# Block-sparse attention and a SwiGLU FFN on one core: all scores on four 32-row tiles, instruction order written by hand, narrower first and last FFN chunks, rms_g applied to x

## The chip, the cores and the metric

The kernel runs on one core of a Trainium2 chip. The metric is the device time of one execution in microseconds (us). Each number below is the median of several executions, and each comparison was made on one chip, with the kernel before run beside the other kernel.

The engines are named as the profile names them. PE is TensorE (matmul), and PEld is its weight load, which overlaps PE. DVE is VectorE, ACT is ScalarE, POOL is GpSimd, and SP is SyncE. "Clock" is the share of full speed that TensorE was granted, as the profile reports it.

## The reference

It is attention over 4 batches, 8 heads, 768 positions and 64 columns. Each query may see only the 6 best blocks of 32 keys. An upper bound built from each block's minimum and maximum ranks the blocks. A gated FFN with RMS norm on 3072 tokens follows.

```python
k_min, k_max = k_chunks.min(axis=3), k_chunks.max(axis=3)           # 24 blocks of 32 keys
ub = sum_d max(q * k_min, q * k_max)                                # causal: later blocks are out
top_chunks = argsort(ub)[..., -6:]
scores = where(selected & causal, q @ k.T / sqrt(64), -1e9)
attn = softmax(scores);  x = (attn @ v) as 3072 x 512
xn = x / rms(x) * rms_g
out = (silu(xn @ w_gate) * (xn @ w_val)) @ w_out                    # 512 -> 1536 -> 512
```

## The kernel before

A *quad* is four heads of one batch (eight quads, numbered 0 to 7). A *unit* is a quad, 256 queries and 256 keys (six per quad, 48 in all). A *slice* is one piece of FFN work: either eight matmuls into `gp` and `vp` and their gating (`gated`), or twelve matmuls into one output tile (`project`). The loop over units puts two slices between the attention steps, so that TensorE has work while the softmax is under way. The parts that matter, cut:

```python
    psS = ... bufs=3 (scores)   psV = ... bufs=1 (values)   psF = ... bufs=4 (FFN and the rest)
    NTILED = NG                     # only quads 0 and 1 use row tiles

    # scores of quads 0 and 1: two heads at a time, each on 32 rows (two halves of d, then the mask)
            for t in range(3):
                for hl in range(2):
                    r = slice(32 * a, 32 * (a + 1))
                    nc.tensor.matmul(o[...], kb_[r, t, ks], qb_[r, t, qs:qs + qn], ...)
    # scores of quads 2 to 7: 88 rows a head (64 of d, 24 of the mask); moved there by DMA
                for dh in range(2):
                    for a in range(4):
                        nc.sync.dma_start(out=dst[bi][32 * dh:32 * (dh + 1), a, :],
                                          in_=hb[32 * a:32 * (a + 1), dh, :])

    # the FFN: chunks of 512 tokens; w_gate and w_val are scaled by rms_g once (fold_g)
    def gated(ht):
        gp = psF.tile(...); vp = psF.tile(...)
        ...                                          # 4 matmuls into gp, 4 into vp
        th = tanh(gp / 2)                            # ACT
        vs = vp / 2                                  # ACT
        tg = (th + 1) * gp                           # DVE; then gp's bank is free
        hh = tg * vs                                 # POOL

    # one token tile of 128: Square on ACT, eps and power on POOL, then on DVE
    xs = xnat[tt] * ri            # in rms(tt)
    tp = PE transposes of xs      # in turn(tt), one unit later
    xsT = copy of tp              # ACT
```

In this kernel a scheduler orders the instructions of each engine. `tc.high_priority` raises the normalisation and the gating in that order.

## Time and profile before

The kernel before took 390.35 us, median of three runs (389.7 to 391.21).

| what | before |
|---|---|
| profiled span | 390.0 us |
| PE busy | 326.9 us (84%) |
| PE idle (span less busy) | 63.1 us |
| first FFN matmul | 76.63 us |
| last values matmul of the loop | about 335.5 us |

These lines are from the page of the kernel before. The first gives busy time with its share of the span. The other two cut the span into 40 slices and show PE's busy tenths and its clock in tenths.

```profile
PE 326.9 (84%) x2301; PEld 184.5 (47%) x2336; DVE 207.8 (53%) x463; ACT 218.1 (56%) x437; POOL 187.5 (48%) x245
...
PE   0078569998979946989899998988999999899995
...
PEclk9995855599998985799999998999999999999999
```

TensorE is the busiest engine. There are two soft spots: the first fifth of the span, and slices 15 to 17 (near 150 us), where PE falls to 4 tenths and, behind that, the clock to 5.

The next lines are from the windows view of the same kernel. Each row gives the window, its length, the busy time (and instructions) of PE, PEld, DVE, ACT and POOL, then the clock, the DMA share and GB/s.

```profile
0.00:76.63 76.63, 44.97 (x345) 28.13 (x346) 53.05 (x119) 27.51 (x50) 27.46 (x55) 0.75 0.95 191
60.00:77.00 17.00, 16.79 (x150) 10.46 (x148) 11.87 (x18) 11.66 (x27) 7.00 (x14) 0.50 0.58 123
76.63:335.50 258.87, 232.90 (x1731) 134.29 (x1761) 141.72 (x325) 165.12 (x344) 139.22 (x170) 0.95 0.31 73
140.00:150.00 10.00, 2.39 (x33) 1.32 (x32) 4.14 (x6) 2.26 (x6) 5.24 (x5) 0.68 0.26 72
150.00:160.00 10.00, 8.77 (x62) 5.76 (x62) 3.23 (x8) 8.33 (x19) 5.32 (x9) 0.50 1.08 226
335.50:390.00 54.50, 49.07 (x232) 22.12 (x233) 13.01 (x20) 25.48 (x45) 20.83 (x21) 0.99 0.10 39
```

What PE waited for, from its waits view (total us, times, longest):

```profile
PE ubp L233 <- DVE qT L159: 19.2, 1, 19.2
...
PE sc L330 <- DMA QH_131<-hb: 5.8, 3, 5.5
...
PE vp L420 <- DVE tg L431: 0.8, 1, 0.8
```

The first line is the start, before the first upper bound. The second is the wait for an operand move. The last says that the FFN hardly ever waited for a bank that `tg` must free: 0.8 us in all.

These PE lines from the timeline of the kernel before (start, duration, operation, count) show one unit of two-tile scores:

```profile
86.08 0.39 PE L302 MATMUL sc<-QH_132,KH_129 32*128 32x256 bf16 x4
86.31 0.27 PE L307 MATMUL sc<-QH_132,chunkrow 32*128 32x256 bf16 x2
86.42 0.38 PE L302 MATMUL sc<-QH_132,KH_129 32*128 32x256 bf16 x4
86.64 0.27 PE L307 MATMUL sc<-QH_132,chunkrow 32*128 32x256 bf16 x2
86.84 1.04 PE L420 MATMUL gp<-xsT,wg 128*128 128x512 bf16 x3
```

Twelve matmuls of 256 columns start within 0.76 us (86.08 to 86.84), 63 ns each, and 55 ns inside a run of six (86.64 less 86.42, over four).

### The profile page before, as it was taken

How to read it: one execution, taken by the hardware profiler on the slowest of the kernel's cores; microseconds unless marked ns; L12 is line 12 of the kernel's file. 1: busy time of each engine (PE TensorE's matmuls, PEld its weight loads, DVE VectorE, ACT ScalarE, POOL GpSimd, SP SyncE). 2: the span in 40 equal slices, each digit the busy share in tenths (PEclk: the TensorE clock that was granted, in tenths of full speed). 3: DMA queues.
4: the chain of work that ended last, by engine and by line, in shares of the span. 5: the costliest groups of instructions: out<-in, count | busy, mean ns of one | idle time of the engine just before them, and what ended most of it. 6: DMA issues, size and time to landing. Idle time of an engine off the chain costs nothing.

```text
span 390.0 us, 6576 instructions
## 1 busy us (share of the span) xinstructions
PE 326.9 (84%) x2301; PEld 184.5 (47%) x2336; DVE 207.8 (53%) x463; ACT 218.1 (56%) x437; POOL 187.5 (48%) x245
## 2 busy tenths in 40 slices
PE   0078569998979946989899998988999999899995
PEld 0045346554435633555456544644565555444442
DVE  4959387659562662595648454935263224512320
ACT  1117126646756246757772777646858579644641
POOL 4116514352884144339742675284737326542640
PEclk9995855599998985799999998999999999999999
DMA  8999997301029217801492069013110110002002
GB/s 190 253 214 190 207 197 166 83 0 33 1 63 217 80 45 177 158 11 33 123 173 69 14 179 180 17 48 114 40 42 13 55 54 2 0 29 81 3 20 87
DMA packets 45408, 35.69 MB, mean 92 GB/s; under 512 B 28928, under 2 KB 36160, under 8 KB 45376
## 3 DMA queue, kind: packets, MB, share of 16 engines
q1 hardware_dynamic: 41712, 30.57, 33.4%
q0 software_dynamic: 3664, 4.72, 7.0%
q8 instruction: 18, 0.29, 0.3%
q14 instruction: 14, 0.11, 0.1%
HBM read 28.31 MB, written 6.29 MB: 89 GB/s over the span
## 4 chain that ended last, share of the span: by engine, by line
PE 49%; DVE 16%; POOL 10%; issue 7%; DMA 7%; ACT 6%; SPq 4%; POOLq 0%; DVEq 0%; ACTq 0%
PE op L441 13%; PE gp L420 9%; PE vp L420 9%; PE ubp L233 6%; PE sc L330 4%; PE avn L358 4%; DMA wv<-in_moe_w_val_dram 4%; PE sc L302 3%; POOL hh L436 3%; ACT pt L337 3%; SPq L184 2%; POOL hb L181 2%; DVE qT L159 2%; DVE tg L431 2%; DVE kT L159 2%
## 5 line engine op out<-in xcount | busy, mean ns | idle before, releaser
L337 ACT ACTIVATE pt<-sc 128x384 bf16<-128x384 f32 (+1 forms) x192 | 93.5, 552 | 74.2 <-PE sc L330 41.0
L436 POOL TENSOR_TENSOR hh<-tg,vs 128x512 bf16<-128x512 bf16 x72 | 83.8, 1168 | 57.4 <-ACT vs L429 38.5
L431 DVE SCALAR_TENSOR_TENSOR tg<-th,gp 128x512 bf16<-128x512 bf16 x72 | 49.2, 683 | 69.5 <-ACT th L427 61.9
L420 PE MATMUL vp<-xsT,wv 128*128 128x512 bf16 x283 | 76.1, 384 | 2.2 <-ACT vs L429 1.1
L420 PE MATMUL gp<-xsT,wg 128*128 128x512 bf16 x268 | 74.2, 384 | 2.6 <-issue 0.6
L441 PE MATMUL op<-wo,hh 128*128 128x512 bf16 x278 | 68.0, 385 | 0.8 <-DVE tg L431 0.2
L342 POOL TENSOR_SCALAR_AFFINE_SELECT pt<-pt 128x512 bf16<-128x512 bf16 x48 | 30.6, 639 | 49.3 <-ACT pt L337 49.1
L429 ACT ACTIVATE vs<-vp 128x512 bf16<-128x512 f32 x72 | 43.0, 598 | 16.3 <-PE vp L420 14.8
L427 ACT ACTIVATE th<-gp 128x512 bf16<-128x512 f32 x72 | 43.3, 601 | 12.2 <-PE gp L420 11.4
L358 PEld LDWEIGHTS <-pt 128*128 128x128 bf16 x672 | 31.9, 103 | 28.9 <-DVE xnat L374 11.7
L420 PEld LDWEIGHTS <-wv 128*128 128x128 bf16 x288 | 28.2, 99 | 35.6 <-issue 4.7
L441 PEld LDWEIGHTS <-hh 128*128 128x128 bf16 x288 | 27.5, 98 | 29.6 <-issue 1.1
L420 PEld LDWEIGHTS <-wg 128*128 128x128 bf16 x288 | 26.1, 99 | 24.7 <-issue 3.5
L373 DVE RECIPROCAL rden<-avn 128x4 f32<-128x4 f32 x48 | 8.4, 176 | 52.8 <-PE avn L358 52.8
L446 ACT ACTIVATE osb<-op 128x512 f32<-128x512 f32 x24 | 14.3, 605 | 28.5 <-PE op L441 24.0
L233 PE MATMUL ubp<-qT,BD_134 128*128 128x288 f32 x32 | 10.8, 457 | 19.2 <-DVE qT L159 19.2
L159 DVE STREAM_TRANSPOSE kT<-kraw 128x768 f32<-128x768 f32 x16 | 23.9, 1551 | 3.9 <-DMA kraw<-in_k_dram 3.9
L159 DVE STREAM_TRANSPOSE qT<-qraw 128x768 f32<-128x768 f32 x16 | 24.0, 1560 | 2.0 <-POOL hb L181 1.9
L358 PE MATMUL avn<-VX_125,pt 128*128 128x65 bf16 x252 | 14.9, 208 | 10.3 <-DVE xnat L374 7.4
L394 DVE TENSOR_SCALAR xs<-xnat,ri_all 128x512 bf16<-128x512 bf16 x24 | 14.1, 588 | 17.2 <-POOL ri_all L392 17.0
L391 POOL TENSOR_TENSOR ri_all<-ss_all,eps_118 128x1 f32<-128x1 f32 x24 | 4.6, 192 | 37.5 <-ACT junk L386 37.3
L330 PE MATMUL sc<-QH_131,KH_128 88*128 88x256 bf16 x96 | 17.4, 300 | 6.1 <-DMA QH_131<-hb 5.8
(99 smaller groups left out, 436.5 us busy)
## 6 DMA issues: line engine op xcount, KB each, us to landing
kraw<-in_k_dram SPq DMA_DIRECT2D x32, 192.0 KB
qraw<-in_q_dram SPq DMA_DIRECT2D x32, 192.0 KB
vraw<-in_v_dram SPq DMA_DIRECT2D x32, 192.0 KB
out_dram<-osb SPq DMA_DIRECT2D x24, 256.0 KB
wo<-in_moe_w_out_dram POOLq DMA_DIRECT2D x1, 1536.0 KB, 19.6
wg<-in_moe_w_gate_dram POOLq DMA_DIRECT2D x2, 768.0 KB, 14.2
wv<-in_moe_w_val_dram POOLq DMA_DIRECT2D x2, 768.0 KB, 18.1
KH_130<-hb SPq DMA_DIRECT2D x16, 48.0 KB
```

The source lines that it names most:

```text
L159: nc.vector.transpose(out=st[nm + "T"][:, dh, :].rearrange("p (m r j) -> p m j r", r=32, j=8), in_=st[nm + "raw"][:, :, :, dh, :],)
L233: nc.tensor.matmul(ubp[:, 0:W], bd[:, t, :], rhs, start=(t == 0), stop=(t == 3))
L330: nc.tensor.matmul(sc[hl][:, 256 * e:256 * e + qn], KH[bi][0:KR, a, kb * P:(kb + 1) * P], QH[bi][0:KR, a, qs:qs + qn], start=True, stop=True,)
L337: nc.scalar.activation(out=pt[:, 2 * hp + hl, 0:W], in_=sc[hl][:, 0:W], func=ACT.Exp, scale=SCALE,)
L342: nc.gpsimd.affine_select(out=dg, in_=dg, compare_op=ALU.is_ge, fill=0.0, base=0, pattern=[[0, 4], [1, P]], channel_multiplier=-1,)
L358: nc.tensor.matmul(avn[:, a, :], pts[kg][:, a, off:off + P], vext[:, kb, a, :], start=(kb == 0 and a == 0), stop=(kb == nkb - 1 and a == 3 ...
L420: nc.tensor.matmul(ps[:], w[:, g, ht * P:(ht + 1) * P], x[:, g, :], start=(g == 0), stop=(g == NP - 1),)
L427: nc.scalar.activation(out=th[:], in_=gp[:], func=ACT.Tanh, scale=0.5)
L429: nc.scalar.activation(out=vs[:], in_=vp[:], func=ACT.Copy, scale=0.5)
L431: nc.vector.scalar_tensor_tensor(out=tg[:], in0=th[:], scalar=1.0, in1=gp[:], op0=ALU.add, op1=ALU.mult,)
L436: nc.gpsimd.tensor_tensor(out=hh[ht][:], in0=tg[:], in1=vs[:], op=ALU.mult)
L441: nc.tensor.matmul(op[:], hh[ht][:, t * P:(t + 1) * P], wo[:, ht, :], start=(ht == 0), stop=(ht == NHT - 1),)
```

## The change

The intent: put the scores of all quads on four row tiles at once, so that no operand has to be moved. Write every engine's order out by hand. Start the FFN earlier with a chunk of 256 tokens. Multiply x by rms_g during the eviction of the transposes, so that the first FFN does not wait for scaled weights. The diff, cut to its core (also changed, and not shown: q of quads 0 and 1 is loaded from ScalarE's queue, the ranking is done in two parts, the weights come in thirds, and several pools have other buffer counts):

```diff
+    ctx.enter_context(tc.manual_schedule(engines={
+        ENG.PE, ENG.Activation, ENG.DVE, ENG.Pool, ENG.SP}))
-    psS = ... bufs=3 ... [P, 512]           # three banks of scores
-    psF = ... bufs=4
+    psS = ... bufs=2 ... [P, 2, 512]        # four banks of scores, one for each head
+    psF = ... bufs=3
     # scores, all quads
-                for hl in range(2):
+                for a in range(4):
                     r = slice(32 * a, 32 * (a + 1))
+                    o = sc[a // 2][:, a % 2, 256 * e:256 * e + q1 - qs]
-    (88-row scores and the DMA moves of k, q and the mask: gone)
-    exponentials: one a head     + exponentials: one for two heads (1024 or 768 columns)
-    CW = 512
+    CHUNKS = [(0, 256)] + [(256 + 512 * i, 512) for i in range(5)] + [(2816, 256)]
-    nc.scalar.activation(out=xsT[c][:, :, o:o + P], in_=tp[:], func=ACT.Copy)
+    nc.vector.tensor_tensor(out=xsT[c][:, :, o:o + P], in0=tp[:],
+        in1=rmsg[:].unsqueeze(2).to_broadcast([P, NP, P]), op=ALU.mult)
-    fold_g(...)                              # gone
+    # the loop: slices are generators; their parts are written between the attention steps
+        scores(nxt)
+        sl = Slice();  sl.part();  exps(nxt, 0);  prep();  sl.part();  exps(nxt, 1);  sl.part();  sl.part()
+        values(u, 0, ...)
+        if last: done.append(normalise(u, 0, avn))
+        sl = Slice();  sl.part();  prep();  sl.part();  sl.part();  sl.part()
+        for f in late: f()                   # turn(): PE transposes, eviction on DVE
+        if last:
+            values(u, 1, ...);  done.append(normalise(u, 1, avn))
+            if quads[qd]["g"] == NG - 1:
+                for tt in done: rms(tt)      # ACT Square, POOL eps and power
+                for tt in done:
+                    xs = scale_x(tt)         # DVE, written right here
+                    late.append(lambda tt=tt, xs=xs: turn(tt, xs))
```

The trade of banks has a reason in the Trainium skill, page "TensorEngine Tiling (Array Packing)", "Gotcha 1: PSUM Pressure": different row tiles must not use one PSUM bank at the same moment. Four tiles at once therefore take four banks, and one comes from the FFN. The kernel keeps to that.

## The prediction

> **What bounds it now.** TensorE. The busy table gives PE 84%, DVE 53%, ACT 56%, POOL 48%; the chain that ended last is 49% PE. Three stretches cost the rest. (1) Start: the first exponential is at 29.5 us (timeline). (2) From 30 to 77 us only attention runs: VectorE waits for weights it scales with rms_g (wv at 47 us), and the windows show PE clock 0.50 from 50 to 77 us; FFN starts at 77.5. (3) Around 140-150 us PE is busy 2.4 of 10 us, ending with scores waiting 5.5 us for QH, an operand move (waits view); the next 10 us run at clock 0.50. From 340 us PE runs FFN gap-free: 0.865 us per four 512-column matmuls, 2.6 us per output tile.
>
> **What changes, costed.**
> - Scores. Before, an 88-row unit is 8 matmuls of 256 columns, about 0.108 us each: 0.87 us at full clock. After, it is 24 matmuls on four row tiles. On two tiles the trace shows 12 in 0.66-0.75 us at full clock (86.1-86.8 us), 55 ns each: two tiles overlap fully. Estimate for four: 0.7-0.9 us a unit. The Trainium skill, "TensorE: Matmul & The Clock Gate", Part 3, gives 3.07x for four row tiles: about 0.84 us. So PE saves little in quads 2-7, roughly 5 us in quads 0-1, where heads went in pairs.
> - Removed: all KH/QH moves with their waits (item 3, about 10 us with the slow clock), copies of chunk rows (6.7 us DVE), folding of rms_g (7.5 us DVE plus its weight wait).
> - ACT: exponentials merge in pairs; 495 and 608 ns for 384 and 512 columns leave an estimated 0.15 us fixed cost: 96 fewer save 15 us. xsT evictions (14 us) move to DVE.
> - FFN columns stay (about 186 us of PE). The first chunk of 256 lets FFN start after unit 4.
> - Risk: psF falls from four banks to three. In the tail a 512 chunk still fits (tg frees gp's bank at 365.8; it is needed at 365.98); the last 256 chunk should stall 2-3 us.
>
> **Where the time comes from.** Start: k and q now load at once; only blocks 6-15 are ranked before the first scores: first exponential about 26 us. Units 0-4 at half clock wait for quad 1's preparation on DVE: first FFN matmul about 50 us. Then, by PE sums: FFN in the loop 140, scores 30-36, values 20 (33 ns each, 24 in 0.78 us), upper bounds 23 (3.88 a quad), transposes 6: about 222. Units 12, 21, 30 and 31 find the FFN queue empty: about 2.5 us of latency each. The tail is 30 slices, 49 us, and 4 us for the last eviction and store. Sum 52+222+10+53 = 337; with 4% of in-order stalls in the loop, 346 us.
>
> **What would show it.** First gp matmul near 50 us; no DMA among PE's releasers; score matmuls starting about 30-40 ns apart; PE clock 0.9 or more after 55 us; exponentials 96 at about 1.0 us; loop end near 293 us, with PE over 90% busy between.
>
> **What would make it wrong.** Four-row tiles that serialise on weight loads (over 1.2 us a unit: +15 us); a hand order that blocks PE on tg or vs with three banks, or on VectorE, which I estimate 77% busy in the loop (27 of 35 us a quad) (+20 us); a slow clock after each unit without FFN.
>
> 346 us; 8 in 10 between 333 and 364. Faster 0.94, same 0.04, slower 0.02.

## More of the kernel before

From 60 to 77 us PE is busy for 16.79 of 17 us and still runs at half clock. From 140 to 150 us it works for only 2.39 us, and the next ten run at half clock. Lines of the PE timeline around this stretch (start, duration, operation, count; brackets give the idle time before an instruction and what ended it):

```profile
129.73 2.75 PE L441 MATMUL op<-wo,hh 128*128 128x512 bf16 x12
...
148.93 1.08 PE L330 MATMUL sc<-QH_131,KH_128 88*128 88x256 bf16 x4 [5.46 <-DMA QH_131<-hb]
...
159.84 0.59 PE L420 MATMUL gp<-xsT,wg 128*128 128x512 bf16 x1
```

From 132.48 (129.73 + 2.75) to 159.84 us there is no FFN matmul at all. By a count through the code, the queue of FFN slices is empty in units 15 to 19.

## The result

The changed kernel took 369.68 us (median of four runs, 367.56 to 370.41), against 390.02 us (389.34 to 391.21) for the kernel before in the same rounds. The ratio is 0.9466, with a 95% interval of 0.9421 to 0.9512. The change is faster, but the gain is 20 us instead of the predicted 44, and the time lies above the predicted range.

The same lines of the page, for the kernel after:

```profile
PE 305.6 (83%) x2971; PEld 177.6 (48%) x3008; DVE 209.8 (57%) x512; ACT 201.7 (55%) x341; POOL 190.8 (52%) x255
...
PE   0076757899699999597999967979999899999995
...
PEclk9996856999699999889999998989999999999999
```

The busy share of PE hardly moved, from 84 to 83%. PE's busy time fell by 21.3 us (326.9 to 305.6), and its idle time is 63.1 us in both (390.0 less 326.9, and 368.7 less 305.6). So the whole gain is a shorter busy time of TensorE (its mean clock rose too, from 0.916 to 0.939), and nothing at all of its idle time. The Trainium skill, "Trainium Kernel Development and Optimization", "Performance Expectations", warns that matmul busy time is a bad metric for the distance to the limit. The share fell by a point while the time fell by 5%.

The windows view of the kernel after, columns as before:

```profile
0.00:56.77 56.77, 24.91 (x268) 16.30 (x269) 39.62 (x97) 19.50 (x22) 25.45 (x46) 0.83 1.14 203
56.77:313.30 256.53, 231.09 (x2435) 135.19 (x2468) 154.43 (x386) 154.12 (x262) 141.94 (x181) 0.95 0.29 66
...
96.00:100.00 4.00, 3.82 (x24) 2.76 (x28) 0.86 (x2) 0.00 (x0) 1.54 (x2) 0.50 1.10 210
152.00:156.00 4.00, 1.19 (x25) 0.78 (x24) 4.00 (x6) 0.81 (x1) 1.68 (x2) 0.65 1.10 232
156.00:160.00 4.00, 3.78 (x17) 1.62 (x16) 2.36 (x4) 1.90 (x3) 1.25 (x3) 0.50 1.05 218
174.00:178.00 4.00, 3.95 (x51) 2.65 (x51) 2.23 (x5) 1.04 (x3) 2.91 (x4) 1.00 0.00 0
...
229.00:233.00 4.00, 3.78 (x41) 1.90 (x35) 2.29 (x4) 2.12 (x4) 2.12 (x3) 0.66 0.00 0
...
245.00:249.00 4.00, 3.62 (x9) 2.00 (x9) 1.43 (x4) 0.79 (x2) 4.00 (x4) 0.57 0.01 2
...
313.30:368.70 55.40, 49.58 (x274) 26.11 (x274) 15.74 (x30) 28.08 (x59) 23.45 (x28) 1.00 0.09 34
```

Against the kernel before, the part until the first FFN matmul is 19.9 us shorter (76.63 to 56.77, PE busy 44.97 to 24.91), the loop 2.3 us shorter and the tail 0.9 us longer. This says where the time is missing, not what took it away: the run with six chunks below starts its FFN 11.3 us later and is as fast.

The ledger against the prediction's sum (spans of the profiled execution, which are about 1.7 us below the device time):

| part | predicted | measured | difference |
|---|---|---|---|
| until the first FFN matmul | 52 | 56.8 | +4.8 |
| loop, PE busy | 222 | 231.1 | +9.1 |
| loop, PE idle | 10 (units without FFN) + 9 (in-order stalls) | 25.4 | +6.4 |
| tail | 53 | 55.4 | +2.4 |
| sum | 346 | 368.7 | +22.7 |

What PE waited for in the kernel after, from its waits view:

```profile
PE ubp L208 <- DVE qT L151: 21.9, 2, 19.3
PE vp L385 <- DVE tg L397: 10.9, 8, 2.2
PE gp L385 <- DVE xsT L368: 6.7, 3, 2.8
...
PE ubp L208 <- POOL qraw L193: 3.6, 2, 2.9
```

No DMA is left among the causes. Instead PE waits 10.9 us for `tg` to free a bank, where it had waited 0.8. Another 8.8 us of the loop (the lines of 6.7 and 3.6, less 1.49 us that stand before the very first FFN matmul) fall where the FFN queue has run empty. Why was `tg` late? These DVE lines come from the timeline of the kernel after; brackets as above:

```profile
167.57 0.42 DVE L330 TENSOR_TENSOR xnat<-avn,rden 128x256 bf16<-128x256 f32 x1
169.56 0.35 DVE L353 TENSOR_SCALAR xs<-xnat,ri_all 128x512 bf16<-128x512 bf16 x1 [1.56 <-POOL ri_all L349]
170.36 0.35 DVE L353 TENSOR_SCALAR xs<-xnat,ri_all 128x512 bf16<-128x512 bf16 x1 [0.45 <-POOL ri_all L349]
170.63 1.09 DVE L151 STREAM_TRANSPOSE qT<-qraw 128x512 f32<-128x512 f32 x1
171.58 0.67 DVE L397 SCALAR_TENSOR_TENSOR tg<-th,gp 128x512 bf16<-128x512 bf16 x1
```

The PE timeline of the same kernel then has:

```profile
172.30 1.02 PE L385 MATMUL vp<-xsT,wv 128*128 128x512 bf16 x4 [2.22 <-DVE tg L397]
```

The `xs` of two token tiles is written straight behind the normalisation. It needs 1/rms, which has to go through ACT (Square) and POOL (two steps), so VectorE stands for 1.56 and 0.45 us. A long transpose and `tg` stand behind it. The input of `tg` had been ready since about 170.2 us (its tanh started on ACT at 169.63 and took 0.59), and PE waits 2.22 us for the bank. The Trainium skill, "TensorE: Matmul & The Clock Gate", "Architectural detail: the array is 16× 32×32, not 1× 128×128", says that ACT and DVE are strict FIFO. These lines agree: an instruction whose data was there did not pass one that waited.

VectorE's own waits view gives the total of this:

```profile
DVE xs L353 <- POOL ri_all L349: 21.3, 23, 1.9
```

The scores, by contrast, did what was promised. PE timeline of the kernel after:

```profile
61.27 0.40 PE L276 MATMUL sc<-qb,kb 32*128 32x256 bf16 x8
61.50 0.28 PE L281 MATMUL sc<-mt,chunkrow 32*128 32x256 bf16 x4
61.61 0.39 PE L276 MATMUL sc<-qb,kb 32*128 32x256 bf16 x8
61.83 0.28 PE L281 MATMUL sc<-mt,chunkrow 32*128 32x256 bf16 x4
62.04 0.61 PE L385 MATMUL gp<-xsT,wg 128*128 128x256 bf16 x4
```

A unit of 24 matmuls takes 0.77 us (61.27 to 62.04), and within a group they start 28 ns apart (0.34 us from 61.27 to 61.61, over twelve).

### The profile page after: what moved, and what is told of

It is laid out like the page before. It is cut to its first block, busy times and chain, and to the rows that moved or that the text cites. A ratio compares the mean times of both kernels' runs of the same rounds, so it can differ in the third digit from the quotient of the medians.

```text
span 368.7 us, 7718 instructions
## 1 busy us (share of the span) xinstructions
PE 305.6 (83%) x2971; PEld 177.6 (48%) x3008; DVE 209.8 (57%) x512; ACT 201.7 (55%) x341; POOL 190.8 (52%) x255
## 4 chain that ended last, share of the span: by engine, by line
PE 58%; DVE 13%; DMA 10%; POOL 6%; ACT 6%; issue 4%; SPq 2%; DVEq 0%; ACTq 0%; POOLq 0%
PE op L408 17%; PE vp L385 11%; PE gp L385 11%; PE ubp L208 9%; DMA kraw<-in_k_dram 8%; PE sc L276 4%; DVE qT L151 4%; PE avn L314 3%; POOL hh L402 3%; DVE tg L397 3%; DVE kT L151 2%; ACT vs L394 2%; DMA vraw<-in_v_dram 2%; POOL ri_all L349 2%; PE sc L281 2%
## 5 line engine op out<-in xcount | busy, mean ns | idle before, releaser
L402 POOL TENSOR_TENSOR hh<-tg,vs 128x512 bf16<-128x512 bf16 (+1 forms) x84 | 86.0, 1026 | 65.1 <-ACT vs L394 48.5
L294 ACT ACTIVATE pt<-sc 128x768 bf16<-128x768 f32 (+1 forms) x96 | 85.9, 913 | 43.2 <-PE sc L281 42.8
L385 PE MATMUL vp<-xsT,wv 128*128 128x512 bf16 (+1 forms) x334 | 78.6, 358 | 12.3 <-DVE tg L397 10.9
L397 DVE SCALAR_TENSOR_TENSOR tg<-th,gp 128x512 bf16<-128x512 bf16 (+1 forms) x84 | 51.0, 607 | 64.3 <-ACT th L391 63.9
L385 PE MATMUL gp<-xsT,wg 128*128 128x512 bf16 (+1 forms) x312 | 77.0, 357 | 8.8 <-DVE xsT L368 6.7
L391 ACT ACTIVATE th<-gp 128x512 bf16<-128x512 f32 (+1 forms) x84 | 45.3, 539 | 23.6 <-PE gp L385 22.7
L394 ACT ACTIVATE vs<-vp 128x512 bf16<-128x512 f32 (+1 forms) x84 | 45.3, 540 | 23.2 <-PE vp L385 18.7
L415 ACT ACTIVATE osb<-op 128x512 f32<-128x512 f32 x24 | 14.3, 597 | 43.2 <-PE op L408 40.3
L276 PE MATMUL sc<-qb,kb 32*128 32x256 bf16 (+1 forms) x768 | 34.8, 270 | 2.1 <-ACT pt L294 2.1
L281 PE MATMUL sc<-mt,chunkrow 32*128 32x256 bf16 (+2 forms) x384 | 25.0, 259 | 0.6 <-DVE mt L237 0.6
L151 DVE STREAM_TRANSPOSE qT<-qraw 128x512 f32<-128x512 f32 x24 | 24.8, 1097 | 0.0
L353 DVE TENSOR_SCALAR xs<-xnat,ri_all 128x512 bf16<-128x512 bf16 x24 | 9.9, 413 | 21.3 <-POOL ri_all L349 21.3
```

Source lines behind the costliest of these rows:

```text
L151: nc.vector.transpose(out=st[nm + "T"].rearrange("p h (m r j) -> p m j h r", r=32, j=8)[:, m], in_=st[nm + "raw"][:, m],)
L276: nc.tensor.matmul(o, st["kb"][r, t, ks], st["qb"][r, t, qs:q1], start=(t == 0), stop=False, skip_group_check=True,)
L281: nc.tensor.matmul(o[:, ms - qs:], chunkrow[r, ks], st["mt"][r, ms:q1], start=False, stop=True, skip_group_check=True,)
L294: nc.scalar.activation(out=pt[:, hs, 0:W], in_=u["sc"][hp][:, :, 0:W], func=ACT.Exp, scale=SCALE)
L385: nc.tensor.matmul(ps[:, 0:W], w[:, g, ht * P:(ht + 1) * P], x[:, g, 0:W], start=(g == 0), stop=(g == NP - 1),)
L391: nc.scalar.activation(out=th[:, 0:W], in_=gp[:, 0:W], func=ACT.Tanh, scale=0.5)
```

## The experiments

The theories for the missing 23 us:

1. VectorE blocks itself: `xs` is written too early and holds up everything behind it, `tg` above all.
2. Three FFN banks are too few, whatever the order.
3. The FFN queue runs empty in units 12, 21, 30 and 31; PE idles there, and the clock falls to one half for a while.

Other runs test parts of the change by themselves. Every kernel gave a correct result. Twelve ran, in three calls; the kernel before took 389.88, 389.48 and 389.42 us in them (medians).

### xs later (theory 1)

The scaling of x is written in the next unit, behind its first slice, when 1/rms has long been there. Nothing else changes.

```diff
         sl.part()
         sl.part()
+        scaled = [(tt, scale_x(tt)) for tt in late]
         ...
-        for f in late:
-            f()
+        for tt, xs in scaled:
+            turn(tt, xs)
         ...
-                for tt in done:
-                    xs = scale_x(tt)
-                    late.append(lambda tt=tt, xs=xs: turn(tt, xs))
+                late = done
```

> Changed kernel, one move: the multiplication of x by 1/rms is written on VectorE after the next unit's first tg instead of right behind the normalisation. Theory 1 (VectorE is blocked in order: xs waits for the ScalarE-GpSimd rms chain while tg stands behind it): PE's waits for tg fall from 10.9 us to under 3 us, VectorE's 21 us of waits for ri_all to under 8, the clock dips after 226 and 245 us go, and the time falls by 8 to 14 us to about 356-362. Theory 2 (three PSUM banks instead of four): the waits for tg stay at 8 us or more and the time within 3 us of 369.7. Theory 3 (units without FFN): also within 3 us.

Measured: 355.39 us, ratio 0.9104 (0.9075 to 0.9133), which is 14.3 us less than the changed kernel. From PE's waits view of this kernel:

```profile
PE vp L385 <- DVE tg L397: 4.7, 6, 1.6
```

And from VectorE's:

```profile
DVE xs L353 <- POOL ri_all L349: 1.9, 3, 0.8
```

VectorE's wait for 1/rms fell from 21.3 to 1.9 us and PE's for `tg` from 10.9 to 4.7, still with three banks. Theory 1 is shown. (The expectation missed in part: the wait stayed above 3 us, and the time fell a little below 356.) What is left of the wait is not VectorE's order at the one place looked at: before PE's wait of 0.98 us (ending at 164.85) `tg` starts at 164.11, 0.1 us after its tanh ended (163.42 + 0.59). The gain is more than PE's wait for `tg` alone: in the loop PE's idle time fell from 25.4 to 14.4 us, and its busy time from 231.1 to 227.4 us, while the mean clock rose from 0.95 to 0.98.

### Fewer units without FFN work (theory 3)

Four slices are held back from units that have another, so that the queue does not run empty so soon at the end of a chunk. The expectation says that all four empty units then have a slice. By a count through the code it is three: units 28 and 29 each give one up, but unit 30 takes both, and unit 31 stays empty.

```diff
-        def __init__(self):
+        def __init__(self, take=True):    # with take=False the slice gets no work
+    HOLD = {11, 20, 28, 29}
-        sl = Slice()                      # the unit's second slice
+        sl = Slice(i not in HOLD)
```

> Changed kernel, one change: units 11, 20, 28 and 29 take one FFN slice instead of two, so that units 12, 21, 30 and 31, which had none, have one each. Theory 3 (the empty FFN queue): the waits of 2.9, 2.8 and 2.4 us near 93, 153 and 215 us and the half clock near 97-102 and 152-159 us go, time down by 7 to 12 us. Theory 1 alone: those waits are short of work, so some is covered, but the four waits of about 2.2 us for tg stay, at most 4 us gained. Theory 2: no change, or worse by up to 2 us because FFN banks are now also wanted in these units.

Measured: 359.76 us, ratio 0.9235 (0.9176 to 0.9293), a gain of 9.9 us. The clock line of this kernel's page:

```profile
PEclk9996856999999999999999999999999999999999
```

Behind the start there is not one dip left. In the loop PE's busy time fell from 231.1 to 225.0 us at a clock of 0.99, and its idle time from 25.4 to 20.8 us. The wait in unit 31 is still there, and so are the waits for `tg` (11.0 us). Lines of this kernel's PE timeline and windows view:

```profile
208.16 1.02 PE L385 MATMUL gp<-xsT,wg 128*128 128x512 bf16 x4 [2.40 <-DVE xsT L368]
...
235.39:239.00 3.61, 3.61 (x25) 2.50 (x25) 1.22 (x4) 0.60 (x1) 3.61 (x4) 1.00 0.01 2
```

So the waits of the two kinds are separate, but the clock is not. In the changed kernel two waits for `tg`, of 2.16 and 2.23 us (ending at 226.71 and 245.38), were followed by a low clock (the windows from 229 and 245 us above). Here the same two waits, of 2.15 and 2.22 us (ending at 218.29 and 235.39), are followed by full clock, though nothing about them was changed. By an estimate from those two windows (3.78 us at 0.66 and 3.62 us at 0.57) this is about 3 of the 9.9 us, and it is luck as far as these runs show. Theory 3 is shown in its direction: filling three of the four units pays. How much of the 9.9 us belongs to it is not separated.

The Trainium skill, "TensorE: Matmul & The Clock Gate", "What's actually happening", puts the fall to half speed behind one idle window of about 3.4 us. The windows of the kernel after, shown above, agree in kind. But recorded waits of 2.85 us (ending at 96.18), 2.81 us (ending at 155.42) and 2.23 us (ending at 245.38) were enough, while those of 2.22 us (ending at 172.30) and 2.40 us (ending at 216.57) were followed by full clock. So the length of one wait does not settle it here.

### Both repairs

Both edits together, nothing else.

> Changed kernel with both repairs (late xs, and one FFN slice in each unit that had none). Alone they gave 14 and 10 us. If they repair different waits, the sum is about 346-349 us, which is what the prediction had called 346 us with 4% of stalls. If they repair the same waits and clock dips twice over, it stays at 352-355 us.

Measured: 350.81 us (349.74 to 352.1), ratio 0.8993 (0.8933 to 0.9054). This beats both kernels and is the best version found. The repairs gain 14.3 and 9.9 us alone and 18.9 together, so they share about 5 us. The clock fits that: with `xs` later alone, unit 12 kept full clock without any FFN work (its wait was 1.42 instead of 2.85 us), and with the held slices alone the dips behind the waits for `tg` were gone. The loop in its windows view:

```profile
55.58:293.90 238.32, 226.28 (x2469) 132.34 (x2469) 155.50 (x386) 154.95 (x263) 142.57 (x181) 0.99 0.32 72
```

The loop takes 238.3 us, where the prediction had 241 (222 + 10 + 9). PE is busy 95% of it.

### The same kernel without the written order

`manual_schedule` is taken out, and nothing else is changed. A scheduler then orders the instructions, from this order of emission.

```diff
-    ctx.enter_context(tc.manual_schedule(engines={
-        ENG.PE, ENG.Activation, ENG.DVE, ENG.Pool, ENG.SP}))
```

> Changed kernel without the written order: the scheduler orders the instructions again, all else (four row tiles, chunks, three FFN banks) kept. If the written order itself brought most of the gain, the time goes back to 380 us or more. If the gain came from the tiles and the missing operand moves, it stays within 7 us of 369.7. If the written order costs through blocking (theory 1), it is faster than 366 us and PE's waits for tg are shorter than 10.9 us.

Measured: 406.11 us, ratio 1.0393 (1.0353 to 1.0432), slower than the kernel before. Some of it is the start: between 30 and 60 us PE is busy 10.87 us (20.14 in the changed kernel), and one upper bound waits 14.3 us for POOL. Some is in the loop, where `vp` waits 11.4 us for ACT's `vs`. This program lacks the priorities of the kernel before, so it does not tell which order is better in general. It does tell that, ordered like this, the other parts of the change do not pay, and that the written order is worth 36 us on this text. Under a scheduler with the priorities of the kernel before they were not tested.

### The kernel before with two-tile scores for all quads

This removes the operand moves from the kernel before, and with them its 88-row scores: the score matmuls of quads 2 to 7 change too. It asks whether their wait is what brings the slow clock near 150 us.

```diff
-    NTILED = NG
+    NTILED = B * NG
```

> Kernel before, one change: all eight quads use the tiled scores, two heads at a time, so no operand is moved by DMA (the casts go to ScalarE as in quads 0 and 1). By the rate of 55 ns a matmul on two tiles, 36 units cost 0.45 us more each on PE, 16 us; the wait of 5.5 us for QH, the half clock behind it and the shorter waits give back about 10 us. Expected 385 to 400 us. If it is below 382 us, the moves cost more than I counted and are most of the change's gain.

Measured: 420.17 us, ratio 1.0773 (1.0736 to 1.0809). The expectation missed. PE's busy time rose from 326.9 to 364.4 us, so two tiles at a time cost far more than the waits they save. A row of its windows view:

```profile
150.00:160.00 10.00, 9.91 (x96) 6.43 (x92) 2.61 (x9) 5.51 (x13) 5.28 (x10) 0.50 0.50 105
```

No DMA is among PE's releasers, PE is busy for 9.91 of the ten us from 150 us on (7.49 in the ten before), and the clock is still 0.50. So slow clock comes here without a single operand move, and the moves are at least not the only cause that the prediction's third stretch can have. What the two kernels share in this stretch is the empty queue: here no FFN matmul runs from 134.18 to 162.23 us, in the kernel before none from 132.48 to 159.84. No run gave the kernel before FFN work in these units, so the share of the moves stays open.

### The kernel before with rms_g on x

The folding of the weights goes, and the eviction multiplies on DVE, as in the change.

```diff
-        nc.scalar.activation(out=xsT[c][:, :, o:o + P], in_=tp[:], func=ACT.Copy)
+        nc.vector.tensor_tensor(out=xsT[c][:, :, o:o + P], in0=tp[:],
+            in1=rmsg[:].unsqueeze(2).to_broadcast([P, NP, P]), op=ALU.mult)
-    folds = [(wg, 0), (wv, 0), (wg, 1), (wv, 1)]
+    folds = []
```

> Kernel before with rms_g applied to x when xsT leaves PSUM (on VectorE, as in the changed kernel) and no folding of the weights. VectorE's wait for wv to land at 47 us (2.3 us, after 3.9 us behind a cast) goes and so do 7.5 us of its work; but FFN still starts only when the first 512 tokens are done. Expected 383 to 390 us: 0 to 7 us gained.

Measured: 385.82 us, ratio 0.9912 (0.9843 to 0.9981): about 3.6 us gained, as expected. The first `gp` starts at 74.37 us instead of 76.63, so the weights' scaling held the FFN back by little more than 2 us.

### The kernel before with three FFN banks (theory 2)

```diff
-    psF = ctx.enter_context(tc.tile_pool(name="psF", bufs=4, ...))
+    psF = ctx.enter_context(tc.tile_pool(name="psF", bufs=3, ...))
```

> Kernel before with three FFN banks instead of four, nothing else. Theory 2 (the fourth bank is worth much): 396 us or more. If three banks are enough with dense FFN slices, as the tail's timing says (bank free at 365.84, needed at 365.98), it stays within 4 us of 390.

Measured: 395.4 us, ratio 1.014 (1.0075 to 1.0205), about 6 us slower: clear of zero, but unclear by the 2% rule, and between the two expectations. PE's waits for `tg` rose: before `vp` from 0.8 to 3.4 us, before `gp` from 0.3 to 2.4, before transposes from 1.4 to 3.9. In the order of the kernel before, the lost bank has a price, but it is less than half of the 14.3 us that the place of `xs` cost. What it costs in the changed kernel itself was not measured: four banks for scores, one for values and four for the FFN would be nine, and both kernels' pools have eight. Theory 2 holds for a small part, and stays open in its size.

### The order of the four tiles, and their separation

First, the same 24 matmuls without a gap, but heads 0 and 1 with all their terms and then heads 2 and 3:

```diff
-            for t in range(3):
-                for a in range(4):
+            for hp, t, hl in [(x, y, z) for x in range(2) for y in range(3) for z in range(2)]:
+                    a = 2 * hp + hl
```

> Changed kernel with the same score matmuls issued for two row tiles at a time instead of four. By the rates in the traces (28 ns a matmul on four tiles, 55 ns on two) 24 matmuls cost 1.32 us instead of 0.67 us a unit, 48 units: up to 31 us more on PE; some of it fills time in which PE waits, so 388 to 400 us. If it stays below 378 us, the four-wide issue is not what makes the change pay.

Measured: 370.64 us, ratio 0.9512 (0.9458 to 0.9566), the same as the change within a microsecond. The expectation missed. Lines of its PE timeline:

```profile
106.08 0.41 PE L277 MATMUL sc<-qb,kb 32*128 32x256 bf16 x8
...
106.86 0.60 PE L386 MATMUL gp<-xsT,wg 128*128 128x512 bf16 x2
```

The 24 matmuls still take 0.78 us. The order inside the group doesn't matter.

Second, the two pairs apart: heads 0 and 1 before the FFN slice, heads 2 and 3 behind its matmuls, as the kernel before had them in quads 0 and 1.

```diff
-            scores(nxt)
+            scores(nxt, 0)
         sl = Slice()
         sl.part()
+        if nxt:
+            scores(nxt, 1)
```

> Changed kernel, the 24 score matmuls of a unit kept as they are, but heads 0-1 come before the FFN slice and heads 2-3 behind it. The run with pairs in adjacent order kept 28 ns a matmul, so adjacency does not matter; theory: what matters is that all four row tiles have work waiting at the same time. Then each half runs at 55 ns a matmul (0.66 us for twelve), 0.65 us more a unit, 31 us in all, of which the waits of PE may hide some: 388 to 400 us. Rival: matmuls of row tiles overlap FFN matmuls too, or the rate is set by something else: within 4 us of 369.7.

Measured: 396.61 us, ratio 1.0158 (1.0076 to 1.024), as expected. Lines of its PE timeline:

```profile
116.20 0.39 PE L277 MATMUL sc<-qb,kb 32*128 32x256 bf16 x4
...
116.97 0.30 PE L315 MATMUL avn<-VX,pt 128*128 128x65 bf16 x4
```

Twelve matmuls now take 0.77 us, as long as 24 did. PE's busy time is 341.4 us instead of 305.6. So having all four tiles in one uninterrupted group is worth 27 us (396.6 less 369.7). Beside the written order it is the largest of the pieces tested; without it the rest is no faster than the kernel before (the 1.6% by which it is slower is unclear by the 2% rule).

### Six chunks of 512

```diff
-    CHUNKS = [(0, 256)] + [(256 + 512 * i, 512) for i in range(5)] + [(2816, 256)]
+    CHUNKS = [(512 * i, 512) for i in range(6)]
```

> Changed kernel with six FFN chunks of 512 tokens instead of 256, 5x512, 256. FFN starts two units later, and more units find the queue empty (units 5 and 6, 15 to 19 and their like), so the half clock spreads; against it, 24 fewer and longer slices and no stalls of 0.26 us in the last chunk. Expected 374 to 384 us; if it is within 3 us of 369.7, the narrow first chunk was worth nothing.

Measured: 367.52 us, ratio 0.9451 (0.9384 to 0.9517). This is indistinguishable from the changed kernel, so the expectation missed: the narrow chunks are worth nothing here. The FFN starts 11.3 us later (68.09 instead of 56.77 us), and still the last values matmuls start at 310.21 us, against 312.55. Most of the 11.3 us is work moved and not saved: until the first FFN matmul PE is busy for 33.98 us here and 24.91 us in the changed kernel, and in the loop for 222.68 and 231.09 us. PE's idle time is 2.2 us longer here before the first FFN matmul, and 3.2 us shorter in the loop. That FFN slices used earlier are missing later fits this, but is argued from the sums.

### Two attempts at a faster start

To the best version, steps of the preparation at the start are reordered (the second half of quad 0's ranking first, the conversion of quad 1's values to bf16 later), with four empty steps behind it:

```diff
-        lambda: (p_half(1, "q", nc.scalar), p_upper(1, 0)),
+        lambda: (p_rank(0, 1), p_choose(0, 1), p_half(1, "q", nc.scalar), p_upper(1, 0)),
         lambda: (p_rank(1, 0), p_upper(1, 1)),
         lambda: p_choose(1, 0),
+        lambda: p_values(1),
         lambda: None,
-        lambda: (p_rank(0, 1), p_choose(0, 1)),
         lambda: (p_rank(1, 1), p_choose(1, 1)),
-    ]
+    ] + [lambda: None] * 4
```

> As the run with both repairs, with the start reordered: blocks 16-23 of quad 0 are ranked in VectorE's idle time at 33-37 us, the cast of quad 1's values leaves the way of the first causal mask, and quad 2's preparation starts two units later, so VectorE has no transposes of quad 2 in front of the normalisations of units 3 and 4. Theory: the first FFN matmul moves from 56.8 us to 50-52 us and the time falls by 3 to 6 us against both repairs. Rival: the start is bound by the DMA (0-65 us it is full) or by PE at half clock; then the first FFN matmul stays after 55 us and the time within 2 us.

Measured: 352.33 us, ratio 0.904 (0.8993 to 0.9087). The first FFN matmul came 3.2 us earlier (52.37 instead of 55.58), and the total did not fall. Between 190 and 200 us PE is busy 6.84 us at a clock of 0.71: the gain was given back there.

The second attempt has two empty steps instead of four, and the last two token tiles are scaled behind one slice of their own:

```diff
-    ] + [lambda: None] * 4
+    ] + [lambda: None] * 2
     ...
+    sl = Slice()
+    for _ in range(4):
+        sl.part()
+    late = [(tt, scale_x(tt)) for tt in late]
```

> As the run with both repairs, with the part of the reordered start that only fills VectorE's idle time, quad 2's preparation one unit later instead of two, and the last two blocks of x scaled behind one FFN slice. The first FFN matmul should be near 53 us and the waits of 1.3 and 0.8 us before the last transposes gone: 346 to 350 us. If it is no faster than 350.8 us, the start is not what bounds the rest.

Measured: 355.98 us, ratio 0.9141 (0.9088 to 0.9194), 5 us slower than the version without it, against the expectation. The start is again early (52.62 us), but PE now waits 4.3 us before `gp` and 4.1 us before `vp` for `tg`, in many short waits of up to 1 us. A likely reason is that the preparation's upper bounds now take other banks of the three in rotation. That is argued from the trace and not tested, so it stays open.

## Why the prediction was right or wrong

**The direction was right, and so were most of the parts.** The first exponential came at 26.83 us (26 predicted; 29.48 before). Scores on four tiles took 0.77 us a unit (0.7 to 0.9 predicted), and matmuls start 28 ns apart (30 to 40 predicted). DMA is gone from PE's waits behind the start. The merged exponentials take 1019 and 807 ns (about 1.0 us predicted).

**The step that failed** is the prediction's "with 4% of in-order stalls in the loop", together with the PE sum it was put on, "222". The stalls were sized at 9 us. Beside the units without FFN they measured 16.6 us (25.4 less 8.8): 10.9 for `tg` and 5.7 for the rest. In addition the sum contained no slow clock, which in the loop came behind two waits in units without FFN and behind two waits for `tg`: PE's work was 231.1 us at a mean clock of 0.95, and 226.3 us at 0.99 once both repairs were in, so about 5 us of the 9 extra are slow clock and 4 us a sum that was too small. The prediction had named the mechanism among the things that would make it wrong: "a hand order that blocks PE on tg or vs with three banks, or on VectorE", and "a slow clock after each unit without FFN". What it did not do was follow `xs` in the order of VectorE: it stands right behind the normalisation, two engines away from its input, and 23 waits of about 0.9 us follow from reading that one line. That order could have been read before the run. It was the order and not the load: the prediction feared a VectorE that is 77% busy in the loop, and it was 60% (154.43 of 256.53 us). Writing `xs` later, and nothing else, gained 14.3 us.

**The start** was set at 52 us and measured 56.8. VectorE's preparation of quad 2 stands ahead of the steps that the first chunk needs. But the attempts show that an earlier start was worth nothing in the total, so this term of the sum does not add as the prediction thought. The same holds for "the first chunk of 256 lets FFN start after unit 4": it does, and six chunks of 512 are as fast.

**Units without FFN** were sized well as waits (10 us predicted, 8.8 measured). Their clock was left out. Holding back four slices fills three of the four units and gains 9.9 us, a part of it from dips behind the waits for `tg`.

**A reading of the kernel before was incomplete.** The prediction laid the slow stretch near 150 us to the operand moves. Their wait of 5.46 us is there, but so is an FFN queue that is empty from 132.48 to 159.84 us. With all moves gone (and the scores on two tiles) the clock is still 0.50 from 150 to 160 us, and in the changed kernel, which has no moves, it is 0.50 from 156 to 160 us behind an empty unit. How much the moves alone cost stays open. The three-bank risk, feared "in the tail", cost almost nothing there (PE's recorded waits in the tail sum to 0.5 us, where 2 to 3 were expected), and about 6 us when the kernel before gave up its fourth bank.

**A check on the sum.** With the two repairs the kernel takes 350.8 us, within 5 us of the predicted 346 and inside its range. The prediction in effect described the kernel that the change would have been with `xs` one step later and a queue that runs empty less often. A part of this agreement is luck, because errors cancel: in the loop PE's busy time is 4.3 us above the 222, and its idle time of 12.0 us is 7 us below the 19.

## What to carry to other kernels

When an order is written by hand, walk down each in-order engine and ask of every instruction through how many other engines its input must still come; place one that crosses two engines a full step later, since everything behind it pays. Work that fills another stage's gaps is a stock: starting it earlier gains nothing if it then runs out, so spread it, and count the clock as well as the idle time where it does. Small-row matmuls should be issued in one uninterrupted group that covers all four row tiles; splitting the group cost 27 us here, the order inside it nothing.

## What the Trainium skill lacked or had wrong

- "TensorE: Matmul & The Clock Gate", "What's actually happening": it has sustained busy work of about 3.4 us bring full clock. In the kernel before PE was busy 16.79 of 17 us (60 to 77 us) with scores, values and upper bounds, and the clock stayed at 0.50 throughout; in the two-tile run it was 0.50 with PE busy 9.91 of 10 us (150 to 160 us). The section lacks that such work can stay at half clock until FFN matmuls come back (in the kernel before 0.70 from 77 to 80 us, then full).
- The same section: one idle window of about 3.4 us is given for the fall. Here PE waits of 2.85 and 2.81 us were followed by 0.50 and one of 2.23 us by 0.57, but waits of 2.22 and 2.40 us by 1.00. With `xs` later, a wait of 1.58 us (ending at 63.57) was followed by 0.69 until 69 us.
- The same page, "Measured speedup vs the span model": 3.07x for four row tiles of 512 columns. In a stream of 24 with 256 columns the starts were 28 ns apart, against 110 ns for full-height matmuls of 256 columns (four in 0.44 us, 62.04 to 62.48), so about 3.9x (3.4x over the whole unit, 0.77 us for 24). The page's figure is for another width, so this is no contradiction. The page does not say that the group has to be uninterrupted (two tiles apart: 55 ns) or that the order in it is free.
- The same page, "Back-to-back issue gap": it gives 131 ns a matmul as the sustained rate for 512 columns. In the tail of the kernel before, four took 0.865 us at full clock, which is 216 ns each; its formula for the isolated gap, which it calls too high for a stream, gives the same 216 ns. The page is at odds with itself here: under "Wait — 56ns, not 53.3ns?" it gives 215.7 ns for back-to-back matmuls.
- No page used tells how to find head-of-line blocking in an in-order engine from a trace. "Perfetto Trace Analysis", "Optimization Strategy", tells to find the gaps of the engine in question and what blocks it, which leads to `tg` here, but it does not go on to what stands ahead of `tg` in VectorE's own queue. VectorE's waits on one line (21.3 us over 23 times) and PE's on another (10.9 us) belonged to one cause.
